# Column sums of V's weights on DMA transposes and GpSimd instead of TensorE, V of blocks 0 to 3 from raw rows, and the third block of x loaded ahead of z2's weights

## The chip, the core and the metric

The kernel runs on one core of a Trainium2 chip. The core has five engines with their own instruction queues: TensorE (PE, matmuls, with PEld as its weight loads), VectorE (DVE), ScalarE (ACT), GpSimd (POOL) and SyncE (SP, which here only issues DMAs). Each queue runs in the order in which it was written; queues are tied together by semaphores. The metric is device time in microseconds of one launch, the median of several runs.

## The reference

Two branches read the same layer-normalized input; both are added to x. S is 2048 rows, D 512, 32 heads of 16; branch A attends to 8 rows at distance 0, 2, ... 14.

```python
def _A_ref(x, wqkv, wo):
    qkv = (x @ wqkv).reshape(B, S, 3, H, Dh).transpose(2, 0, 3, 1, 4)
    q, k, v = (qkv[0], qkv[1], qkv[2])
    ...
    logits = jnp.einsum('bhsd,bhswd->bhsw', q, kg) * scale
    logits = jnp.where(mask[None, None, :, :], logits, -1000000000.0)
    attn = _softmax(logits, axis=-1)
    o = jnp.einsum('bhsw,bhswd->bhsd', attn, vg)
    return o.transpose(0, 2, 1, 3).reshape(B, S, D) @ wo

def _B_ref(x, w_in, w_sp, b_sp, w_out):
    z = _gelu(jnp.einsum('bsd,df->bsf', x, w_in))
    z1 = z[..., :Fh].copy()
    z2 = _layernorm(z[..., Fh:], axis=-1)
    g = jnp.einsum('ts,bsf->btf', w_sp, z2) + b_sp[None, :, None]
    return jnp.einsum('bsf,fd->bsd', z1 * g, w_out)
x = A_x
xn = _layernorm(x, axis=-1)
return x + _A_ref(xn, A_wqkv, A_wo) + _B_ref(xn, B_w_in, B_w_sp, B_b_sp, B_w_out)
```

V can be had without the normalized rows: with W the V columns of wqkv, m and r the mean and the reciprocal deviation of a row, (x - m) r W = r (x W) - m r (column sums of W). The kernel uses this for the first blocks.

## The kernel before

**How it is built.** The program is a list of tasks. Each task names its engine, an estimate of its duration, a priority and what it reads and writes; dependencies follow from that (and from overlaps of memory, since buffers share places in one SBUF arena). `Plan.schedule` lays all tasks out by a model with those estimates (a matmul by columns, a DMA by bytes, landing times of the first loads from a table `land`), always picking the task that can start first, and by priority among those within `tol`. The order that comes out is written to each engine's queue and is fixed: on the chip a task that is not ready holds up all behind it. `overlap` is what the model takes off every DVE operation. A hand-written chain (L1003 to L1012) fixes the order of the opening on PE, DVE and ACT.

**How it is tiled.** The 2048 rows are 16 blocks of 128 and 4 stages of 512 (index j or tc).

- x blocks are loaded (L514, L541); DVE takes each block's statistics (L599, L601, L609), GpSimd the power -1/2 (`rstd`, L611), DVE normalizes (L623). The transpose of the normalized block goes through PE and an ACT copy for blocks 0 to 3 (`xTr`, L579, and `xTe`, L587), and through a DMA transpose on SP for blocks 4 to 15 (L617).
- V (`v_block`, L645): 4 matmuls of 512 columns a block (L654). Blocks 0 and 1 take x raw: transposed on PE (`xTx`, L579), copied by ACT (`xTc`, L606), multiplied, then corrected by the column sums (`fix`, DVE, L660, in place in PSUM) and scaled by r on eviction (`Ve`, ACT, L663). The column sums come from four matmuls with a matrix of ones (`colsum`, L638) and one negating eviction to all partitions (L642). V goes from a slot (`Vn`, 8 slots, block b uses slot b mod 8) to a DRAM buffer by a store on POOL's queue (`Vw`, L668), and comes back gathered at 8 distances in the attention (L930).
- z2 (`z2_block`): 8 matmuls of 448 columns a block (L766), in two halves, as the weights are loaded in two halves (L524, L530). Gelu (L774) and sum of squares (L779) on ACT. `z2_wave` normalizes four blocks at a time: small DVE operations (L785 to L792), the power -1/2 on GpSimd (L795), and DVE's scaling (L798).
- Q and K (`qk_pair`, L677, evictions L686); products of Q with shifted K and their sums on DVE (L698, L703); the reduction over heads on PE (L713) for two stages at once, softmax on DVE and ACT (L725 to L752).
- z1 (L812, gelu L818 into `z1T`), the mixing with w_sp (L907, with w_sp transposed by DMA on SP, L880), attention times V on DVE (L935 to L941), its transposes (L944), and the output (L963, L972, L978, L983).

**Order around the change.** Loads at the start: x0 and x1 on ACT's queue; on SP the V weights in two halves, x2, z2's weights in two halves, x3 to x7, Q's and K's weights, x8 to x15. PE starts with eight matmuls on constants (L560), then the hand-written order.

Of the kernel before, what the change touches and what calls it, by code (L numbers as in the profile page):

```python
# [36 lines left out]
class Plan:  # L37
# [85 lines left out]
    def schedule(self, dma_bw=300.0, xbar_bw=190.0, dma_lat=1300.0, dma_pre=400.0, issue=None, tol=40.0, land=None,  # L123
# [49 lines left out]
        while left:  # L173
# [43 lines left out]
            if t.dma is not None:  # L217
                iss = issue[e]
                t.eng_end = r + iss
                bw = xbar_bw if t.dma.get("xbar") else dma_bw  # L220
                xs = max(r + iss + dma_pre, dma_free)
                xe = xs + t.dma["nbytes"] / (bw if xs > 7000.0 else min(bw, 265.0))
                dma_free = xe
                t.end = xe + dma_lat
                if t.name in land:
                    t.end = land[t.name]
                    dma_free = land[t.name] - 500.0
            else:
                dur = t.est
                if t.tbl is not None:  # L230
                    if tbl is not None and t.tbl != tbl:
                        dur += 1300.0
                    tbl = t.tbl
                t.end = r + dur
                t.eng_end = t.end - (overlap if e == "dve" else 0.0)
# [103 lines left out]
def build_kernel(nc, A_x, A_wqkv, A_wo, B_x, B_w_in, B_w_sp, B_b_sp, B_w_out, out, report=False, emit=True):  # L339
# [12 lines left out]
    NWARM = 8  # L352
# [3 lines left out]
    vscr = nc.dram_tensor("vscr", (16 + S, 512), BF).ap()  # L356

# [4 lines left out]
    def place(size, **names):  # L362
        for k, o_ in names.items():
            off[k] = top[0] + o_
        top[0] += size
# [5 lines left out]
    place(3584, w_in1=0, tg=0, On=2048, xcT=0, ncs=1024)  # L371
# [8 lines left out]
    off["xn"] = off["attn"]  # L380
    AR = top[0]
# [4 lines left out]
    for name, n in (("prime", 4), ("mx", 128), ("Zb", 256), ("Z", 128), ("maskt", 128), ("st6", NB * 6),  # L386
                    ("mv", NB * 2), ("vpe", NB), ("rstd", NB), ("s1", NB), ("s2", NB), ("m2", NB), ("msq", NB),
                    ("vpe2", NB), ("rstd2", NB), ("mhalf", 4)):
        foff[name] = fb
        fb += n  # L390
# [5 lines left out]
    with ExitStack() as es:  # L396
# [59 lines left out]
        for s_ in range(2):  # L456
            R1(("wv", s_), "wv", 1024, 1024 * s_)
# [8 lines left out]
        for hf in range(2):  # L466
            for b in range(2):
                R1(("xcT", b, hf), "xcT", 256, 512 * b + 256 * hf)
            R(("xnT", 0, hf), "sb", [(off["xnT"] + dc * S, off["xnT"] + dc * S + 128) for dc in (2 * hf, 2 * hf + 1)])
        R1("ncs", "ncs", 1024)  # L470
# [6 lines left out]
        def c_mm(n):  # L477
            return max(26.0, n / 2.4 + 2.7)
# [12 lines left out]
        def dma(eng, fn, nbytes, chan, reads=(), writes=(), name="", xbar=False, prio=0.0, after=()):  # L491
            return T(eng, fn, reads=reads, writes=writes, name=name, prio=prio, after=after,
                     dma=dict(chan=chan, nbytes=nbytes, xbar=xbar))
# [7 lines left out]
        ncs = A("ncs", 1024).bitcast(F32)  # L501
# [15 lines left out]
        def ld_wv(hf):  # L517
            dma("sp", lambda e: e.dma_start(AC(off["wv"] + 1024 * hf, [[512, 2], [1, 512]]),  # L518
                                            A_wqkv[256 * hf:256 * hf + 256, 1024:1536].rearrange("(c p) n -> p c n",
                                                                                               p=128)),  # L520
                256 * 512 * 2, ("wv", hf), writes=[("wv", hf)], name="ldwv%d" % hf)
# [13 lines left out]
        def ld_wqk(which, eng):  # L535
# [5 lines left out]
        dma("act", lambda e: e.dma_start(A("xin", 512), x2[0:128, :]), 128 * 512 * 2, ("xin", 0),  # L541
            writes=[("xin0", 0), ("xin0", 1)], name="ldx0")
        ld_x(1, "act")
        ld_wv(0)
        ld_wv(1)
        ld_x(2, "sp")
        ld_win2a()
        ld_win2b()
        ld_x(3, "sp")
# [23 lines left out]
        def pe_tr(src, keys, name):  # L573
            bk = plan.bank(name)

            def tr(t):
                last = None
                for dc in range(4):
                    last = t.matmul(P(bk, 128, 128 * dc), src[:, 128 * dc:128 * dc + 128], ident, start=True,  # L579
                                    stop=True)  # L580
                return last
            T("pe", tr, reads=keys + ["ident"], writes=[bk], est=(430.0 if name == "xTx0" else 4 * c_mm(128)), name=name)
            return bk
# [9 lines left out]
        def ln_block(b):  # L593
# [9 lines left out]
            if b < 2:  # L603
                bc = pe_tr(xin, xk, "xTx%d" % b)
                for hf in range(2):
                    T("act", (lambda hf: lambda a: a.activation(A("xcT", 256, 512 * b + 256 * hf), P(bc, 256, 256 * hf),  # L606
                                                                ACTF.Copy))(hf),
                      reads=[bc], writes=[("xcT", b, hf)], est=c_act(256), name="xTc%d_%d" % (b, hf), prio=-1)
# [22 lines left out]

        def colsum():
            bk = plan.bank("cs")
            for hf in range(2):
                def mm(t, hf=hf):
                    last = None
                    for dc in (2 * hf, 2 * hf + 1):
                        last = t.matmul(P(bk, 512), ones[:, 0:128], A("wv", 512, 512 * dc), start=(dc == 0),  # L638
                                        stop=(dc == 3))
                    return last  # L640
                T("pe", mm, reads=[("wv", hf)], writes=[bk], est=2 * c_mm(512) * (1 if hf else 2), name="cs_%d" % hf, prio=2)
            T("act", lambda a: a.activation(ncs, P(bk, 512), ACTF.Copy, scale=-1.0), reads=[bk],  # L642
              writes=["ncs"], est=c_act(512), name="cse", prio=-0.5)

        def v_block(b):  # L645
# [4 lines left out]
            for hf in range(2):  # L650
                def mm(t, hf=hf):
                    last = None
                    for dc in (2 * hf, 2 * hf + 1):
                        last = t.matmul(P(bk, 512), A("xcT", 128, 512 * b + 128 * dc) if b < 2 else xTv(b, dc),  # L654
                                        A("wv", 512, 512 * dc), start=(dc == 0), stop=(dc == 3))
                    return last
                T("pe", mm, reads=[("xcT", b, hf) if b < 2 else ("xnT", b), ("wv", hf)], writes=[bk],
                  est=2 * c_mm(512) * (1.5 if (b, hf) == (0, 0) else 1), name="V%d_%d" % (b, hf), prio=(2 if b < 4 else 60 + b))
            if b < 2:
                T("dve", lambda v: v.scalar_tensor_tensor(P(bk, 512), ncs, Fv("mv", 1, 2 * b), P(bk, 512),  # L660
                                                          ALU.mult, ALU.add),
                  reads=["ncs", ("mv", b)], writes=[bk], est=690, name="fix%d" % b, prio=1)
            T("act", lambda a: a.activation(vn.rearrange("p (d h) -> p d h", d=16),  # L663
                                            PC(bk.col(), [[1, 16], [16, 32]]), ACTF.Copy,
                                            scale=Fv("rstd", 1, b) if b < 2 else 1.0),
              reads=[bk] + ([("rstd", b)] if b < 2 else []), writes=[("Vn", sl)], est=c_act(512), name="Ve%d" % b,
              prio=4)
# [158 lines left out]
        lnd = [ln_block(b) for b in range(2)]  # L826
        colsum()
        v_block(0)
        v_block(1)
        lnd += [ln_block(b) for b in range(2, NB)]  # L830
# [18 lines left out]
        for b in range(2, NB):  # L849
            v_block(b)  # L850
# [152 lines left out]
        for names in (["warm%d" % wi for wi in range(NWARM)] +  # L1003
                      ["xTx0", "cs_0", "V0_0", "xTx1", "cs_1", "V0_1", "xTr0", "V1_0", "xTr1", "V1_1",
                       "z2_0_0", "z2_0_0b", "z2_0_1", "xTr2", "z2_1_0", "z2_1_1", "V2_0", "V2_1", "xTr3", "z2_2_0"],
                      ("rstd4", "Vw0"),
                      ("bnst0", "bnag0", "vpe0", "bnst1", "bnag1", "vpe1", "norm0", "norm1", "bnst2", "bnag2",
                       "vpe2", "norm2", "fix0", "bnst3", "bnag3", "vpe3", "fix1", "norm3", "bnst4", "bnag4", "vpe4",
                       "bnst5"),
                      ["bnst%d" % b for b in range(5, NB)],  # L1010
                      ("xTc0_0", "xTc0_1", "xTc1_0", "xTc1_1", "xTe0_0", "xTe0_2", "cse", "xTe1_0", "xTe2_0", "z2g0",
                       "Ve0", "xTe3_0", "z2g1", "Ve1", "Ve2", "z2s0"), ("V10_1", "Q3_3")):  # L1012
            for n0, n1 in zip(names, names[1:]):
                if byname[n0] not in byname[n1].deps:
                    byname[n1].odeps.add(byname[n0])

        plan.schedule(tol=50.0, dma_bw=300.0, dma_lat=1600.0, overlap=40.0,
                      land=dict(ldx0=3580.0, ldx1=4700.0, ldwv0=4050.0, ldwv1=5300.0, ldx2=5700.0, ldwin2a=6950.0, ldwin2b=8250.0,
                                ldx3=8650.0, ldx4=9050.0, ldx5=9400.0, ldx6=9750.0, ldx7=10200.0, ldq=11700.0, ldk=13200.0))
# [50 lines left out]
```

## Time and profile before

| what | us |
|---|---|
| runs (three) | 237.56, 237.21, 237.30; median 237.3 |
| the profiled execution's span | 236.1 |
| PE busy | 231.7 (98%) |
| DVE busy | 207.4 (88%) |
| ACT busy | 96.5 (41%) |
| POOL busy | 32.7 (14%) |
| mixing matmuls, L907 | 96.6 |
| Q and K matmuls, L677 | 28.7 |
| z2 matmuls, L766 | 26.0 |
| V matmuls, L654 | 15.6 |

The profile is one execution. A timeline row gives the start, the duration, the engine and line, output and inputs with shapes, the number of merged instructions, and in brackets the idle time before and what ended it. A matmul row's duration runs from the first start to the modelled end of the last; the pace is read from the starts. The granted TensorE clock is full in all 40 slices. The column "to landing" of a DMA counts from its issue. A few matmul records are missing.

### The profile page before, as it was taken

The numbers are of one execution on the slowest core, as the hardware profiler recorded it, in microseconds if no ns is written. First come the engines' busy times: TensorE is split into PE (matmuls) and PEld (weight loads), VectorE is DVE, ScalarE is ACT, GpSimd is POOL, SyncE is SP. The second block draws the span as 40 slices with busy tenths as digits, with TensorE's granted clock in tenths as the row PEclk, the third lists the DMA queues.
The fourth block names the chain that finished last, engine by engine and source line by source line (L and its number), as shares of the span: only waits on it lengthen the run. The fifth ranks groups of instructions, "written<-read, shape, count | busy, mean of one in ns | idle before, by whom it ended". The sixth has DMA issues, their size and how long they took to land.

```text
span 236.1 us, 2974 instructions
## 1 busy us (share of the span) xinstructions
PE 231.7 (98%) x1114; PEld 109.1 (46%) x1135; DVE 207.4 (88%) x269; ACT 96.5 (41%) x145; POOL 32.7 (14%) x56
## 2 busy tenths in 40 slices
PE   8999999999999999999999999999999999999996
PEld 3455555555444444444444444444444444444443
DVE  3799899999998899999699998986989997999432
ACT  3598889888967895510120531111111111000000
POOL 2259650311733100000000000000000000000000
PEclk9999999999999999999999999999999999999999
DMA  7998969991048325430999999998995959936432
GB/s 211 352 283 163 243 146 217 195 202 44 22 165 260 92 85 69 104 118 0 226 347 252 225 266 180 200 304 187 346 258 175 261 161 303 193 95 181 135 96 69
DMA packets 82013, 43.86 MB, mean 186 GB/s; under 512 B 54336, under 2 KB 81360, under 8 KB 82000
## 3 DMA queue, kind: packets, MB, share of 16 engines
q1 hardware_dynamic: 80768, 41.27, 71.5%
q0 software_dynamic: 800, 2.11, 2.8%
q10 hardware_dynamic: 432, 0.30, 0.6%
q8 instruction: 9, 0.15, 0.3%
q14 instruction: 4, 0.03, 0.1%
HBM read 26.35 MB, written 4.21 MB: 129 GB/s over the span
## 4 chain that ended last, share of the span: by engine, by line
PE 94%; DMA 3%; SPq 1%; ACT 1%; issue 1%; DVE 0%
PE ps L907 41%; PE ps L677 12%; PE ps L972 10%; PE ps L812 10%; PE ps L766 9%; PE ps L963 6%; PE ps L654 5%; DMA arena<-in_B_w_in_dram 3%; PE ps L713 1%; ACT arena L774 0%; SPq L518 0%; ACT arena L587 0%; PE ps L579 0%; SPq L514 0%; SPq L524 0%
## 5 line engine op out<-in xcount | busy, mean ns | idle before, releaser
L907 PE MATMUL ps<-arena 128*128 128x512 bf16 x439 | 96.6, 379 | 0.5
L907 PEld LDWEIGHTS ps<-arena 128*128 128x128 bf16 x448 | 43.7, 98 | 53.1 <-issue 0.4
L915 ACT ACTIVATE arena<-ps 128x1024 bf16<-128x1024 f32 (+1 forms) x16 | 14.7, 917 | 78.0 <-PE ps L907 78.0
L698 DVE TENSOR_TENSOR arena<-arena 128x4096 bf16<-128x4096 bf16 x16 | 36.5, 2282 | 0.1
L935 DVE TENSOR_TENSOR arena<-arena 128x4096 bf16<-128x4096 bf16 x16 | 36.4, 2283 | 0.0
L938 DVE TENSOR_TENSOR arena<-arena 128x2048 bf16<-128x2048 bf16 (+1 forms) x32 | 29.9, 948 | 0.0
L677 PE MATMUL ps<-arena 128*128 128x512 bf16 x126 | 28.7, 379 | 0.1
L703 DVE TENSOR_TENSOR arena<-arena 128x4096 bf16<-128x4096 bf16 x12 | 27.4, 2287 | 0.1
L972 PE MATMUL ps<-arena 128*128 128x512 bf16 (+2 forms) x117 | 26.9, 366 | 0.1
L766 PE MATMUL ps<-arena 128*128 128x448 bf16 x128 | 26.0, 352 | 0.5 <-DMA arena<-in_B_w_in_dram 0.5
L812 PE MATMUL ps<-arena 128*128 128x512 bf16 x110 | 24.4, 379 | 0.1
L978 DVE TENSOR_TENSOR arena<-ps,arena 128x512 bf16<-128x512 f32 (+2 forms) x17 | 11.2, 658 | 11.7 <-PE ps L972 11.7
L677 PEld LDWEIGHTS ps<-arena 128*128 128x128 bf16 x128 | 14.5, 113 | 13.0
L766 PEld LDWEIGHTS ps<-arena 128*128 128x128 bf16 x128 | 12.3, 98 | 12.7 <-ACT arena L642 0.7
L686 ACT ACTIVATE arena<-ps 128x1024 bf16<-128x1024 f32 x16 | 16.3, 1021 | 4.4 <-PE ps L677 4.1
L972 PEld LDWEIGHTS ps<-arena 128*128 128x128 bf16 x119 | 11.4, 98 | 12.8
L812 PEld LDWEIGHTS ps<-arena 128*128 128x128 bf16 x112 | 10.9, 98 | 13.2 <-ACT arena L818 0.3
L963 PE MATMUL ps<-arena 128*128 128x512 bf16 (+2 forms) x66 | 16.5, 366 | 0.1
L774 ACT ACTIVATE arena<-ps 128x896 bf16<-128x896 f32 x16 | 14.6, 914 | 3.2 <-PE ps L766 3.1
L818 ACT ACTIVATE arena<-ps 128x1024 bf16<-128x1024 f32 (+1 forms) x16 | 13.9, 923 | 4.9 <-PE ps L812 4.8
L654 PE MATMUL ps<-arena 128*128 128x512 bf16 x60 | 15.6, 379 | 0.2
L779 ACT ACTIVATE arena<-arena 128x896 bf16<-128x896 bf16 x16 | 15.1, 945 | 0.0
(61 smaller groups left out, 168.5 us busy)
## 6 DMA issues: line engine op xcount, KB each, us to landing
arena<-vscr SPq DMA_DIRECT2D x16, 1024.0 KB, 7.1
arena<-in_A_x_dram SPq DMA_DIRECT2D x30, 128.0 KB, 3.6
vscr<-arena POOLq DMA_DIRECT2D x16, 128.0 KB, 3.0
out_dram<-arena SPq DMA_DIRECT2D x15, 128.0 KB, 1.8
arena<-in_A_wqkv_dram SPq DMA_DIRECT2D x2, 512.0 KB, 6.9
arena<-in_B_w_in_dram SPq DMA_DIRECT2D x2, 448.0 KB, 6.1
arena<-in_B_w_in_dram SPq DMA_DIRECT2D x1, 896.0 KB, 5.9
arena<-in_B_w_out_dram SPq DMA_DIRECT2D x1, 896.0 KB, 4.9
```

The lines of the kernel that those rows point to most:

```text
L654: last = t.matmul(P(bk, 512), A("xcT", 128, 512 * b + 128 * dc) if b < 2 else xTv(b, dc), A("wv", 512, 512 * dc), start=(dc == 0), stop=(d ...
L677: last = t.matmul(P(bk, 512, 512 * which), AC(off["wqk"] + 2048 * which + 512 * dc + c, [[4, 128]]), AC(off["xnT"] + dc * S + 512 * j, [[1 ...
L686: T("act", lambda a: a.activation(AC(qo, [[ko - qo, 2], [1, 512]]), P(bk, 1024).rearrange("p (t n) -> p t n", t=2), ACTF.Copy, scale=0.5), ...
L698: T("dve", (lambda pbv, qb, kb: lambda v: v.tensor_tensor(pbv, qb, kb, ALU.mult))(pbv, qb, kb), reads=rd, writes=[("pb", s_)], est=c_tt(40 ...
L703: T("dve", (lambda av, bv: lambda v: v.tensor_tensor(av, av, bv, ALU.add))(av, bv), reads=[("pb", 1)], writes=[("pb", acc)], est=c_tt(4096 ...
L766: last = t.matmul(P(bk, 448, 512 * hf), xTv(b, dc), AC(off["w_in2"] + 896 * dc + 448 * hf, [[1, 448]]), start=(dc == 0), stop=(dc == 3))
L812: last = t.matmul(P(bk, 512, 512 * i), AC(off["w_in1"] + 896 * dc + 128 * fc, [[1, 128]]), AC(off["xnT"] + dc * S + 512 * j, [[1, 512]]), ...
L907: last = t.matmul(P(bk, 512, 512 * i), AC(off["z2"] + FH * sh + 128 * fc, [[1, 128]]), AC(off["wT%d" % r_] + sh * 512, [[1, 512]]), start= ...
L935: T("dve", lambda v: v.tensor_tensor(tv, tv, av, ALU.mult), reads=[("attn", b)], writes=[("Vs", sv)], est=c_tt(4096), name="pv%d" % b, pri ...
L938: T("dve", (lambda n: lambda v: v.tensor_tensor(A("Vs", n, 4096 * sv), A("Vs", n, 4096 * sv), A("Vs", n, 4096 * sv + n), ALU.add))(n), wri ...
L963: last = t.matmul(P(bk, cn), AC(off["OT"] + 512 * tb + 128 * cc, [[1, 128]]), AC(off["wo"] + 512 * cc + c0, [[1, cn]]), start=(cc == 0), s ...
L972: last = t.matmul(P(bk, cn), AC(off["z1T"] + fc * S + 128 * tb, [[1, 128]]), AC(off["w_out"] + 512 * fc + c0, [[1, cn]]), start=False, sto ...
```

## The change

- The column sums: after the twelve DMA transposes of normalized x, SP issues four more that transpose W. GpSimd adds halves nine times (256, 128, ... 1 for each of four groups) to 512 sums, stores them to a DRAM buffer (`csw`, POOL's queue), and SP loads them back to all partitions (`csr`). The matmuls with ones and their eviction are gone.
- V of blocks 0 to 3 (`NRAW`) is taken from raw x. Blocks 0 and 1 are evicted and scaled by DVE, 2 and 3 by ACT, to a float buffer `vraw`; one DVE operation a block (`fix`) later adds the column sums times -m r (`mr`, one small DVE operation) and writes the slot. The stores of V of these blocks come after that.
- The new buffers (`xcT`, `csb`, `vraw`, `wvT`, `cst`) lie in the place of `z1T`.
- Loads: x0 in two halves of rows on SP and ACT; W in three pieces; x3 directly behind x2, ahead of z2's weights. One warm-up matmul fewer.
- PE's hand-written order takes V of blocks 0 to 3 and the transposes of raw blocks 2 and 3 ahead of z2 of block 0; V of blocks 0 and 1 goes matmul by matmul. DVE's and ACT's orders follow.
- The planner: issue time and latency of DMA transposes, `tol` 20 instead of 50, DMA rate 330 instead of 300, `overlap` 20 instead of 40, a new table of landings.

```diff
@@ Plan.schedule
-                t.eng_end = r + iss
+                t.eng_end = r + (t.dma.get("iss") or iss)
...
-                t.end = xe + dma_lat
+                t.end = xe + (900.0 if t.dma.get("xbar") else dma_lat)
@@ build_kernel
-    NWARM = 8
+    NRAW = 4
+    NWARM = 7
...
     off["xn"] = off["attn"]
+    off["xcT"] = off["z1T"]
+    off["csb"] = off["xcT"] + 512 * NRAW
+    off["vraw"] = off["csb"] + 1024
+    off["wvT"] = off["vraw"] + 1024 * NRAW
+    off["cst"] = off["wvT"] + 2048
...
-                     dma=dict(chan=chan, nbytes=nbytes, xbar=xbar))
+                     dma=dict(chan=chan, nbytes=nbytes, xbar=xbar, iss=(1270.0 if nbytes < 400000 else 2200.0) if xbar else None))
...
-        dma("act", lambda e: e.dma_start(A("xin", 512), x2[0:128, :]), 128 * 512 * 2, ("xin", 0),
-            writes=[("xin0", 0), ("xin0", 1)], name="ldx0")
+        for h, q_ in enumerate(("sp", "act")):
+            dma(q_, (lambda h: lambda e: e.dma_start(ar[64 * h:64 * h + 64, off["xin"]:off["xin"] + 512],
+                                                     x2[64 * h:64 * h + 64, :]))(h),
+                64 * 512 * 2, ("xin0", h), writes=[("xin0", h)], name="ldx0%s" % "ab"[h])
         ld_x(1, "act")
-        ld_wv(0)
-        ld_wv(1)
+        for d0, dn in ((0, 1), (1, 1), (2, 2)):
+            ld_wv(d0, dn)
         ld_x(2, "sp")
+        ld_x(3, "sp")
         ld_win2a()
         ld_win2b()
-        ld_x(3, "sp")
@@ ln_block
-            if b < 2:
+            if b < NRAW:
                 bc = pe_tr(xin, xk, "xTx%d" % b)
@@ colsum
-            T("pe", mm, reads=[("wv", hf)], writes=[bk], est=2 * c_mm(512) * (1 if hf else 2), name="cs_%d" % hf, prio=2)
-            T("act", lambda a: a.activation(ncs, P(bk, 512), ACTF.Copy, scale=-1.0), reads=[bk],
-              writes=["ncs"], est=c_act(512), name="cse", prio=-0.5)
+            for dc in range(4):
+                dma("sp", (lambda dc: lambda e: e.dma_start_transpose(AC(off["wvT"] + 128 * dc, [[512, 4], [1, 128]]),
+                                                                      A("wv", 512, 512 * dc)))(dc),
+                    128 * 512 * 2, ("wvT", dc), reads=[("wv", dc)], writes=[("wvT", dc)], name="wvT%d" % dc, xbar=True,
+                    prio=2, after=lnd[4:])
+            n, prev = 256, "wvT"
+            while n:
+                if n == 256:
+                    a_, b_ = (AC(off["wvT"] + o_, [[512, 4], [1, n]]) for o_ in (0, n))
+                else:
+                    a_, b_ = (FT(o_, n) for o_ in (0, n))
+                T("pool", (lambda n, a_, b_: lambda g: g.tensor_tensor(FT(0, n) if n > 1 else Fv("cs", 4).rearrange(
+                    "p (c k) -> p c k", k=1), a_, b_, ALU.add))(n, a_, b_),
+                  reads=[("wvT", dc) for dc in range(4)] if n == 256 else ["cst"] if n == 1 else [],
+                  writes=["cst"] if n > 1 else ["cs"], est=200 + 4.2 * n, name="csum%d" % n, prio=1, after=lnr)
+                n //= 2
+            dma("pool", lambda e: e.dma_start(bass.AP(tensor=cscr.tensor, offset=cscr.offset, ap=[[1, 128], [128, 4]]),
+                                              Fv("cs", 4), allow_slow_non_contiguous=True),
+                2048, "cswr", reads=["cs"], writes=["cscr"], name="csw", prio=1)
+            dma("sp", lambda e: e.dma_start(csb, bass.AP(tensor=cscr.tensor, offset=cscr.offset, ap=[[0, 128], [1, 512]])),
+                128 * 2048, "csrd", reads=["cscr"], writes=["csb"], name="csr", prio=2)
@@ v_block
-            if b < 2:
-                T("dve", lambda v: v.scalar_tensor_tensor(P(bk, 512), ncs, Fv("mv", 1, 2 * b), P(bk, 512),
-                                                          ALU.mult, ALU.add),
-                  reads=["ncs", ("mv", b)], writes=[bk], est=690, name="fix%d" % b, prio=1)
+            if b < NRAW:
+                if b < 2:
+                    T("dve", lambda v: v.tensor_scalar(vraw(b), P(bk, 512), Fv("rstd", 1, b), None, ALU.mult),
+                      reads=[bk, ("rstd", b)], writes=[("vraw", b)], est=680, name="Ve%d" % b, prio=4)
+                else:
+                    T("act", lambda a: a.activation(vraw(b), P(bk, 512), ACTF.Copy, scale=Fv("rstd", 1, b)),
+                      reads=[bk, ("rstd", b)], writes=[("vraw", b)], est=c_act(512), name="Ve%d" % b, prio=4)
+                T("dve", lambda v: v.scalar_tensor_tensor(vdh, hd(csb), Fv("mr", 1, b), hd(vraw(b)), ALU.mult, ALU.add),
+                  reads=["csb", "mr", ("vraw", b)], writes=[("Vn", sl)], est=690, name="fix%d" % b, prio=6)
@@ the hand-written order
-                      ["xTx0", "cs_0", "V0_0", "xTx1", "cs_1", "V0_1", "xTr0", "V1_0", "xTr1", "V1_1",
-                       "z2_0_0", "z2_0_0b", "z2_0_1", "xTr2", "z2_1_0", "z2_1_1", "V2_0", "V2_1", "xTr3", "z2_2_0"],
-                      ("rstd4", "Vw0"),
+                      ["xTx0", "xTx1", "V0_0", "V0_1", "V1_0", "V1_1", "V0_2", "xTx2", "V0_3", "V1_2", "V1_3", "xTx3", "V2_0", "V2_2",
+                       "xTr0", "V3_0", "V3_2", "xTr1", "z2_0_0", "z2_0_0b", "z2_0_1", "xTr2", "z2_1_0", "z2_1_1", "xTr3", "z2_2_0"],
...
-        plan.schedule(tol=50.0, dma_bw=300.0, dma_lat=1600.0, overlap=40.0,
+        plan.schedule(tol=20.0, dma_bw=330.0, dma_lat=1600.0, overlap=20.0,
```

`hd(x)` is a view of 512 values with the head index innermost; `FT(o, n)` is n values at offset o of each of four groups of `cst`, in float.

## The prediction

> **What bounds the kernel now.** First the chain of waits by share, then in order of time; then the waits of TensorE (PE), and the timelines of the five queues.
>
> ```profile
> PE 94%; DMA 3%; SPq 1%; ACT 1%; issue 1%; DVE 0%
> ...
> 2.79 6.50 DMA arena<-in_B_w_in_dram
> ...
> 9.34 0.93 PE ps L766 x4
> ...
> PE ps L766 <- DMA arena<-in_B_w_in_dram: 0.5, 2, 0.3
> ```
>
> The end is set by one load (the second half of z2's weights, landing at 9.3 us) and, from 9.34 us to 234.2 us, by matmuls back to back. PE's only late waits are for that load. So time can be won only ahead of 9.34 us, by having done more by then; and lost anywhere behind it where PE's fixed order meets a task that isn't ready.
>
> ```profile
> 7.34 0.59 PE L654 MATMUL ps<-arena 128*128 128x512 bf16 x2
> 8.22 0.92 PE L766 MATMUL ps<-arena 128*128 128x448 bf16 x4 [0.28 <-DMA arena<-in_B_w_in_dram]
> 9.34 0.93 PE L766 MATMUL ps<-arena 128*128 128x448 bf16 x4 [0.21 <-DMA arena<-in_B_w_in_dram]
> ...
> 12.06 0.81 PE L654 MATMUL ps<-arena 128*128 128x512 bf16 x3
> ...
> 14.45 1.03 PE L654 MATMUL ps<-arena 128*128 128x512 bf16 x4
> ```
>
> These are the opening's PE rows: PE stands idle about 0.45 us ahead of 8.22 and 0.35 us ahead of 9.34, while V of blocks 2 and 3 (12.06 and 14.45; one record of the first is missing) still lies ahead. A 512-column matmul follows the last after 0.216 us (15.31 to 22.22 holds 32 of them), four transposes take 0.22 us (5.38 to 5.60), four z2 matmuls 0.75 us.
>
> **The opening.** Removed: four column-sum matmuls (0.86 us), their eviction on ScalarE (0.60 us, L642) and a 128-column warm-up. Added ahead of z2: raw transposes of blocks 2 and 3 (0.44 us) and their copies (2 x 0.60 us on ScalarE). Moved ahead: V2 and V3, 8 x 0.216 = 1.73 us. If T is the moment z2 of block 0 starts, with all data for the next tasks there, the work left at T is that left at 9.34 before, less 1.73, plus the first half of z2 (0.75). The gain is 9.34 + 1.73 - 0.75 - T = 10.32 - T. For T I walk the new order: x0 comes as two halves on two queues (first transpose at about 3.6, 3.73 before), x1 at 4.4; first copy done 0.65 + 0.3 us behind the transpose's start, as at 3.73/4.38, so V0 at 4.65, V1 at 5.35 once block 1 is copied; V0 and V1 fill the wait for x2 and x3 (to about 6.9); copies of blocks 2 and 3 end near 7.1 and 7.9, so V2 at 7.15 and V3 at 8.2; second normalized transpose to 9.3. Sum of work 1.3 + 3.46 = 4.8 us from 3.6, and 0.9 us of waits: T = 9.3. z2's weights have x3 ahead of them now, 128 KB at the 350 GB/s of those microseconds = 0.37 us: 8.5 and 9.7 us. The second half is needed at 10.06, so they no longer decide. SP issues two more descriptors there (0.46 us each), in front of loads that queue for bandwidth anyway; if landing followed issue, the halves would come at 9.4 and 10.6 and cost 0.5 us. Gain **1.0 us**, bounds 0.4 and 1.3.
>
> **Costed at nothing.** The finer V groups add no matmuls. The V0/V1 evictions on VectorE (DVE; 0.7 us each) stand where two fixes of 0.75 us stood. The four late fixes (4 x 0.75, L660's row) and a 0.16 us product add 3.2 us to DVE around 50 to 62 us; PE's order is made knowing them, and z1's matmuls (23 us of them from 73 us) fill PE meanwhile; at the far end DVE is done 9 us before it must be:
>
> ```profile
> 219.06 0.42 DVE L941 TENSOR_TENSOR arena<-arena 128x512 bf16<-128x512 bf16 x1
> ...
> 231.62 0.81 PE L963 MATMUL ps<-arena 128*128 128x384 bf16 x4
> ```
>
> Without that cover they would cost 3.2 us. The four weight transposes wait behind the twelve of normalized x on SP and push w_sp's transposes back by 4 x 1.3 us, the csr load by 0.5 us more; w_sp's eight end at 50.9 and are read from 98.2 on.
>
> **Where the column sums go.** SP issues the last x transpose at 30 us, then four at 1.3 us: until 36.5, landed about 39.5 (4.3 us from issue, the median of L617). Then nine dependent additions on GpSimd, then a store to DRAM and a broadcast load back. The adds' own time is not in the trace. They have 1024, 512, ... 4 elements per partition, 2044 in all. Low bound: DVE's 128x1024 float row, 1.22 us, so 1.1 ns an element and 0.1 us an instruction: 3.1 us. High: GpSimd's 128x128 select, 0.29 us, of which 0.10 a minimal memset's: 1.5 ns, and 0.3 us an instruction: 5.8 us. I take 4.5 (1.5, 0.9, 0.55, 0.4, and five of 0.25), midway as neither row is an add on GpSimd. The Trainium skill ("GPSIMD Engine Reference", Elementwise — side-by-side cycle accounting) gives 4497 ns for an add of 2048 float elements; by that the nine would take, by my estimate, some 6 us.
>
> But they do not run alone:
>
> ```profile
> 45.34 3.05 POOL L795 TENSOR_TENSOR fpool<-fpool 128x4 f32<-128x4 f32 x1 [10.09 <-DVE fpool L792]
> ...
> 76.62 1.04 POOL L795 TENSOR_TENSOR fpool<-fpool 128x4 f32<-128x4 f32 x1
> ...
> 45.23 2.29 DVE L703 TENSOR_TENSOR arena<-arena 128x4096 bf16<-128x4096 bf16 x1
> ...
> 76.28 1.23 DVE L730 TENSOR_TENSOR arena<-ps,fpool 128x1024 bf16<-128x1024 f32 x1
> ```
>
> The same four-element GpSimd instruction takes 1.04 us beside a DVE operation that reads PSUM, and 3.05 us beside one that reads two tensors of SBUF: 45.34 + 3.05 = 48.39 is 0.87 us behind that DVE operation's end at 47.52. It happens at 32.20 and 61.02 too, and the single rstd at 26.73 (2.53 us instead of 0.55) made DVE wait 0.52 us. From 38 to 63 us DVE does almost nothing but such 2.29 us operations. So each add waits for a boundary between two of them: nine take about 20 us instead of 4.5. The reverse, DVE waiting while GpSimd reads, four elements are too few to show: from nothing (DVE went on at once at 47.55) to all 4.5 us. As one kept the other out of reading, I take it as mutual; four adds fall there before DVE stops for another reason: 1.5 + 0.9 + 0.55 + 0.4 = 3.3 us. The Trainium skill ("SBUF — State Buffer", Who interferes with whom) says so: a DVE instruction with two SBUF inputs and a GpSimd instruction that reads SBUF lock each other out for the whole instruction; the trace agrees for GpSimd's waits, and by the rule the DVE would lose up to 6 us here, by no hold at all 3.3 us less than I sum.
>
> That other reason: L795 of wave 1 stands behind the adds on GpSimd's queue (its inputs came at 45.3, the adds' at 39.5), and DVE's L798 for blocks 4 to 7 waits for it, with the whole chain of products (L698, L703) queued behind. DVE gets there near 49.8 + 3.3 = 53 us; then GpSimd is free of it and finishes five adds (1.25), the store's issue (0.6, a V store's row) and L795 (1.04): **2.9 us** of DVE standing. Bounds: 1.6 if all adds are through, 4.5 if the store's 512 pieces cost four times 128 rows. DVE is then 6.2 us late against the plan.
>
> What is late next is the head reduction, which PE takes the moment it is planned ready:
>
> ```profile
> 60.90 2.29 DVE L703 TENSOR_TENSOR arena<-arena 128x4096 bf16<-128x4096 bf16 x1
> ...
> 64.64 1.05 PE L713 MATMUL ps<-arena 128*32 128x512 bf16 x16
> ```
>
> The last sum ends at 63.19, PE comes at 64.64: 1.45 us of slack; the planner's overlap of 20 instead of 40 ns makes some 40 DVE operations later in the plan, 0.8 us more. PE stands 6.2 - 2.25 = **3.9 us**, and nothing behind gives it back, since PE is full to the end.
>
> **Sum.** Against this execution's span of 236.1: -1.0 + 3.9 = 239.0. The median of the runs, 237.3, lies 1.2 us above that span, so 240.2.
>
> **Rivals.** (A) *The adds stay hidden*: DVE is not held, and loses under 2.25 us. For it: DVE's next operation began on time at 47.55 with a GpSimd instruction still running, and the adds' result isn't wanted till the fixes. Against: L798's place behind L795. Then only the opening counts: 237.3 - 1.0 = 236.3 (236.0 to 236.9). (B) *The fixes become the wait*: store and load back of the sums take 3.0 and 3.7 us (medians of L668 and L518); if the adds run their full 20 us with no stop at L798, they end at 61, the sums are back at 68, and DVE, due at a fix near 60, stands 8 us with 3.3 us lost before: 11.3 - 2.25 = 9 us of PE, 245.3. It decides from a landing later than some 62 us. For it: V8's slots wait for these stores too; against: a stop at L798 lets the adds finish by 54.5. (C) *No gain, no loss*: x3 lands behind 7.2, so V3 and z2 slip by 1 us and the opening's order gives nothing, or PE's stand is just 1 us: 237.3.
>
> **Chances.** Forecast 0.50 (its own range 238.2 to 243.5: lateness of 4 to 8.5 us), A 0.34, B 0.08, C 0.08. A measurement of this kernel can tell 0.2% (0.5 us) from no change: faster 0.34 (A), same 0.08 (C), slower 0.58 (forecast and B). The range 236.0 to 244.5 holds A, C and the forecast, and leaves out B and the tails.
>
> **What would show it.** Opening: V3 ahead of the first L766, which starts near 9.3 with no DMA wait at the second half. Adds: nine GpSimd instructions from 39.5 on, most about 2.3 us apart; DVE operations of 2.3 us stretched or late at the first four. Then DVE idle ahead of L798 of wave 1, released by GpSimd, and a PE gap ahead of L713. If PE has no gap behind 10 us, the forecast is wrong and A holds; if DVE's longest wait is at a fix for the sums' load, B.

## The result, and the profile after

The changed kernel takes 250.13 us (median of four runs, 249.88 to 250.20) against 237.25 us (four runs, 237.06 to 237.56): ratio 1.0538 [1.0525, 1.0552], slower. Its profiled execution has a span of 249.0 us, 12.9 us above that of before (236.1).

The chain of waits of the changed kernel by share, then TensorE's waits (us in total, times, longest):

```profile
PE 72%; DMA 9%; POOL 6%; DVE 6%; SPq 3%; issue 2%; ACT 1%; DVEq 0%; POOLq 0%
```
```profile
PE ps L814 <- ACT arena L714: 7.2, 1, 7.2
PE ps L698 <- ACT arena L714: 2.0, 1, 2.0
PE ps L761 <- DVE arena L751: 1.4, 1, 1.4
```

Before, PE was 94% of the chain and had no late wait. Now it stands three times between 62 and 84 us. L714 is ScalarE's eviction of V (L663 before), L761 the head reduction (L713 before), L751 a head sum (L703 before).

The chain of the changed kernel in order of time (start, length, what):

```profile
37.38 2.54 DMA arena<-arena
...
40.04 3.65 POOL arena L665
...
55.62 0.21 POOL fpool L665
...
56.12 10.10 DMA cscr<-fpool
...
66.24 4.37 DMA arena<-cscr
...
81.07 2.21 DVE arena L751
```

This is the path of the column sums. The last weight transpose lands at 39.92; nine adds, five of 3.65 down to 2.26 us and four of 0.21 to 0.27, end at 55.83; the store of 2 KB to DRAM takes 10.10 us from issue to landing, the load back 4.37; then come the four fixes, what DVE has queued behind them, and the head reduction.

DVE in the timeline of the changed kernel:

```profile
39.42 2.28 DVE L746 TENSOR_TENSOR arena<-arena 128x4096 bf16<-128x4096 bf16 x1
41.74 4.09 DVE L751 TENSOR_TENSOR arena<-arena 128x4096 bf16<-128x4096 bf16 x1
45.76 1.23 DVE L837 TENSOR_SCALAR fpool<-fpool 128x4 f32<-128x4 f32 x1
...
49.10 0.68 DVE L840 TENSOR_TENSOR fpool<-fpool 128x4 f32<-128x4 f32 x1
...
58.16 0.51 DVE L846 TENSOR_SCALAR arena<-arena,fpool 128x896 bf16<-128x896 bf16 x1 [3.72 <-POOL fpool L843]
...
70.63 1.13 DVE L711 SCALAR_TENSOR_TENSOR arena<-arena,fpool 128x512 bf16<-128x512 f32 x1 [6.01 <-DMA arena<-cscr]
```

Three losses of DVE are to be seen. While the adds run, its operations stretch: 4.09 us instead of 2.28, 1.23 instead of 0.17, 0.68 instead of 0.15, and one of 2.43 at 52.02 instead of 2.28: 3.55 us in all. Then it waits 3.72 us for the small power of wave 1 (L843), which stands behind the adds and the store on GpSimd's queue. Then 6.01 us at the first fix, for the sums.

TensorE in the timeline, two of its rows before the change, and the windows around its stands (busy time of PE, PEld, DVE, ACT, POOL, then granted clock, DMA share, GB/s):

```profile
10.29 0.92 PE L814 MATMUL ps<-arena 128*128 128x448 bf16 x4
11.39 0.93 PE L814 MATMUL ps<-arena 128*128 128x448 bf16 x4 [0.19 <-DMA arena<-in_B_w_in_dram]
...
62.52 1.68 PE L814 MATMUL ps<-arena 128*128 128x448 bf16 x8
66.22 1.90 PE L698 MATMUL ps<-arena 128*128 128x512 bf16 x8 [2.02 <-ACT arena L714]
...
78.79 3.17 PE L814 MATMUL ps<-arena 128*128 128x448 bf16 x8 [7.22 <-ACT arena L714]
83.33 1.05 PE L761 MATMUL ps<-arena 128*32 128x512 bf16 x16 [1.37 <-DVE arena L751]
...
87.77 23.47 PE L860 MATMUL ps<-arena 128*128 128x512 bf16 x106
```
```profile
62.17 1.68 PE L766 MATMUL ps<-arena 128*128 128x448 bf16 x8
...
74.92 23.47 PE L812 MATMUL ps<-arena 128*128 128x512 bf16 x106
```
```profile
62.00:66.00 4.00, 2.14 (x11) 0.88 (x9) 2.58 (x2) 1.35 (x2) 0.00 (x0) 1.00 0.00 0
...
74.00:78.00 4.00, 0.00 (x0) 0.00 (x0) 3.97 (x3) 0.60 (x1) 3.44 (x6) 0.65 1.20 306
78.00:82.00 4.00, 3.17 (x8) 1.01 (x8) 4.00 (x6) 3.10 (x6) 1.35 (x3) 0.50 0.67 245
```

The z2 matmuls at 62.52 stood at 62.17 before: all that happens in the first 62 us costs PE 0.35 us. The long run of z1 matmuls, at 74.92 before, starts at 87.77: 12.85 us later, which is the whole of the lost time. So it is lost between 62 and 88 us. The two waits for L714 are ways by which DVE's lateness reaches PE: at 64.65 ScalarE has waited 3.75 us for DVE (L746), with the V eviction queued behind; at 75.78 it has waited 6.72 us for the store of a block that the late fix had to write first, since V's slot is used again:

```profile
75.78 0.60 ACT L714 ACTIVATE arena<-ps 128x512 bf16<-128x512 f32 x1 [6.72 <-DMA vscr<-arena]
```

In the window from 62 to 66 the DMA engines carry nothing, though the store is in flight. After the long stand the granted clock is 0.50, and eight matmuls take 3.17 us instead of 1.68.

DVE's losses add up to this without those waits: 3.55 + 3.72 + 6.01, and the four fixes at 1.07 us where the plan had 0.69 (1.5 in all), are 14.8 us; less the 2.25 us of slack that the prediction worked out 12.5, with the opening's 0.35 some 12.9. No run measures the slack by itself; it is borne out only by the sum.

### The profile page after: what moved, and what is told of

The parts are those of the page before. It is cut to its first block, busy times and chain, and to the rows that moved or that the text cites. A ratio compares the mean times of both kernels' runs of the same rounds, so it can differ in the third digit from the quotient of the medians.

```text
span 249.0 us, 3004 instructions
## 1 busy us (share of the span) xinstructions
PE 233.0 (94%) x1117; PEld 109.1 (44%) x1138; DVE 213.7 (86%) x274; ACT 95.7 (38%) x144; POOL 45.7 (18%) x66
## 4 chain that ended last, share of the span: by engine, by line
PE 72%; DMA 9%; POOL 6%; DVE 6%; SPq 3%; issue 2%; ACT 1%; DVEq 0%; POOLq 0%
PE ps L956 39%; PE ps L860 10%; PE ps L1021 10%; POOL arena L665 6%; PE ps L1012 5%; DMA cscr<-fpool 4%; PE ps L725 3%; PE ps L814 3%; DMA arena<-in_B_w_in_dram 3%; DVE arena L751 2%; DMA arena<-cscr 2%; DVE arena L711 2%; SPq L655 2%; DMA arena<-arena 1%; PE ps L698 1%
## 5 line engine op out<-in xcount | busy, mean ns | idle before, releaser
L746 DVE TENSOR_TENSOR arena<-arena 128x4096 bf16<-128x4096 bf16 x16 | 36.7, 2292 | 0.2
L984 DVE TENSOR_TENSOR arena<-arena 128x4096 bf16<-128x4096 bf16 x16 | 36.3, 2282 | 0.0
L814 PE MATMUL ps<-arena 128*128 128x448 bf16 x128 | 27.5, 366 | 7.5 <-ACT arena L714 7.2
L751 DVE TENSOR_TENSOR arena<-arena 128x4096 bf16<-128x4096 bf16 x12 | 29.1, 2428 | 0.1
L814 PEld LDWEIGHTS ps<-arena 128*128 128x128 bf16 x128 | 12.5, 100 | 20.4 <-ACT arena L714 7.7
L665 POOL TENSOR_TENSOR arena<-arena 128x1024 f32<-128x1024 bf16 (+7 forms) x8 | 15.0, 1869 | 3.0 <-DMA arena<-arena 2.5
```

What stands on the lines that cost most here:

```text
L665: T("pool", (lambda n, a_, b_: lambda g: g.tensor_tensor(FT(0, n) if n > 1 else Fv("cs", 4).rearrange("p (c k) -> p c k", k=1), a_, b_, AL ...
L746: T("dve", (lambda pbv, qb, kb: lambda v: v.tensor_tensor(pbv, qb, kb, ALU.mult))(pbv, qb, kb), reads=rd, writes=[("pb", s_)], est=c_tt(40 ...
L751: T("dve", (lambda av, bv: lambda v: v.tensor_tensor(av, av, bv, ALU.add))(av, bv), reads=[("pb", 1)], writes=[("pb", acc)], est=c_tt(4096 ...
L814: last = t.matmul(P(bk, 448, 512 * hf), xTv(b, dc), AC(off["w_in2"] + 896 * dc + 448 * hf, [[1, 448]]), start=(dc == 0), stop=(dc == 3))
L984: T("dve", lambda v: v.tensor_tensor(tv, tv, av, ALU.mult), reads=[("attn", b)], writes=[("Vs", sv)], est=c_tt(4096), name="pv%d" % b, pri ...
```

## The experiments

All were run beside the kernel before on the same chip. The operations keep their names; line numbers move with the edits. The ratio is worked out over all runs, with a 95% interval; it need not be the quotient of the two medians.

**Column sums by matmul again, all else as changed.** This tells the sums' path from the rest of the change.

```diff
-            for dc in range(4):
-                dma("sp", (lambda dc: lambda e: e.dma_start_transpose(AC(off["wvT"] + 128 * dc, [[512, 4], [1, 128]]),
-                                                                      A("wv", 512, 512 * dc)))(dc),
...
-            n, prev = 256, "wvT"
-            while n:
...
+            bk = plan.bank("cs")
+            for hf in range(2):
+                def mm(t, hf=hf):
+                    last = None
+                    for dc in (2 * hf, 2 * hf + 1):
+                        last = t.matmul(P(bk, 512), ones[:, 0:128], A("wv", 512, 512 * dc), start=(dc == 0),
+                                        stop=(dc == 3))
+                    return last
...
+            T("act", lambda a: a.activation(csb, P(bk, 512), ACTF.Copy), reads=[bk],
+              writes=["csb"], est=c_act(512), name="cse", prio=-0.5)
```

> The changed kernel with its column sums alone undone: four matmuls with ones and one ScalarE copy give them to all partitions; the opening, the raw blocks 0 to 3 and the late fix stay. Theory (the 12.9 us come from the chain weight transposes, GpSimd additions, store, load back): the chain is gone, left are the opening's 0.35 us (matmuls from 62 us on start that much later than before) and up to 0.86 us of matmuls, so 237.5 to 238.5, no PE wait over 1 us behind 12 us. Rival (the late fixes, the shared V slots or the raw blocks themselves cost it): 245 or more.

Measured: 237.82 us against 237.05, ratio 1.0031 [1.0018, 1.0044], span 236.4. TensorE's waits have no row behind the opening. So all but 0.8 of the 12.9 us belong to the new path of the sums. Raw V for four blocks, the late fixes, the new loads, the planner's constants and the four matmuls with ones that are back cost that together, gains and losses set off.

**One DVE reduction for the nine adds.** Takes GpSimd out, keeps the store.

```diff
-            n, prev = 256, "wvT"
-            while n:
...
-                n //= 2
+            T("dve", lambda v: v.tensor_reduce(Fv("cs", 4), A("wvT", 2048).rearrange("p (c n) -> p c n", c=4), AX.X, ALU.add),
+              reads=[("wvT", dc) for dc in range(4)], writes=["cs"], est=2200, name="csum", prio=1)
```

> The nine GpSimd additions are one VectorE reduction of 2048 elements a partition (some 2.2 us); weight transposes, store, load back and late fixes stay. Theory (the additions, kept out of SBUF reads by VectorE's two-input operations, are the first 15.6 us of a chain that is wanted 13 to 14 us earlier): the sums are ready near 42 instead of 55.8, store and load end near 57, where the plan wants them; 237.7 to 239.5, and L843 of wave 1 takes 3.05 us with no wait of VectorE for it over 0.5 us. Rival (store and load set it, whatever comes before): the wait at the first fix stays 5 us or more and the time above 245.

Measured: 244.13 us, 1.0331 [1.0312, 1.0350], span 241.4. DVE's timeline, and the store in the table of DMAs (KB each, us to landing):

```profile
41.05 2.27 DVE L659 TENSOR_REDUCE fpool<-arena 128x4 f32<-128x2048 bf16 x1
...
61.13 1.12 DVE L702 SCALAR_TENSOR_TENSOR arena<-arena,fpool 128x512 bf16<-128x512 f32 x1 [4.52 <-DMA arena<-cscr]
```
```profile
cscr<-fpool POOLq DMA_DIRECT2D x1, 2.0 KB, 12.0
```

The sums are ready at 43.3, 12.5 us earlier, and no operation of DVE is stretched. Still it waits 4.52 us at the fix: the store, issued at 43.6, lands after 12.0 us, and the load comes behind a w_sp transpose on SP's queue at 56.8. So the adds are not all; the store, with a head start of 12 us, still decides. The time lies between what was expected (237.7 to 239.5) and its rival (above 245): the stop for the small power of wave 1 is gone, as expected, and most of the wait at the fix has stayed, as the rival had it.

**The same 2 KB in another layout.** The four sums of a partition go out as one piece of 16 bytes, 128 pieces instead of 512 of 4 bytes; the fix reads them back in that order. The adds stay.

```diff
-            dma("pool", lambda e: e.dma_start(bass.AP(tensor=cscr.tensor, offset=cscr.offset, ap=[[1, 128], [128, 4]]),
-                                              Fv("cs", 4), allow_slow_non_contiguous=True),
+            dma("pool", lambda e: e.dma_start(bass.AP(tensor=cscr.tensor, offset=cscr.offset, ap=[[4, 128], [1, 4]]),
+                                              Fv("cs", 4)),
...
-                T("dve", lambda v: v.scalar_tensor_tensor(vdh, hd(csb), Fv("mr", 1, b), hd(vraw(b)), ALU.mult, ALU.add),
+                T("dve", lambda v: v.scalar_tensor_tensor(
+                    vn.rearrange("p (d a e) -> p d a e", d=16, a=4), csb.rearrange("p (e d a) -> p d a e", e=8, d=16),
+                    Fv("mr", 1, b), vraw(b).rearrange("p (a e d) -> p d a e", a=4, e=8), ALU.mult, ALU.add),
```

> As the changed kernel, but the sums are stored as 128 pieces of 16 bytes instead of 512 of 4, and the fix reads them in that order. Theory (each link of the chain counts in full, as it is wanted at 57 and comes at 70.6): if the pieces are what makes the store take 10.1 us, it lands in some 3.5 us, VectorE's 6.0 us wait at the first fix goes, and the time falls by 6 to 7 us to 243 to 244.5. Rival (the store queues behind w_sp's transposes, its form is nothing): 249 to 250.5.

Measured: 245.27 us, 1.0332 [1.0305, 1.0360], span 242.7. The store's row and DVE's timeline:

```profile
cscr<-fpool POOLq DMA_DIRECT2D x1, 2.0 KB, 1.9
```
```profile
57.73 0.51 DVE L848 TENSOR_SCALAR arena<-arena,fpool 128x896 bf16<-128x896 bf16 x1 [3.51 <-POOL fpool L845]
...
64.10 1.08 DVE L711 SCALAR_TENSOR_TENSOR arena<-arena,fpool 128x512 bf16<-128x512 f32 x1
```

1.9 us instead of 10.1, and the fix waits for nothing. What is left are the forecast's own steps: DVE held 3.55 us, 3.51 us at L848 (L798 of before), PE 3.65 us at the head reduction. So the layout of a 2 KB store is worth 6.3 us of span and 4.9 us of the median. The median lies above the 243 to 244.5 that were expected; the profiled execution took 243.91, the other three 245.19 to 245.36 at a lower mean clock (0.993 instead of 1.00).

**Slots of their own for V of blocks 0 to 3.** TensorE's longest wait is named by V's slots; is that a cause, or a way?

```diff
-            vn = A("Vn" if sl < 4 else "bbc", 512, 512 * (sl % 4))
+            vn = A("xcT", 512, 512 * b) if b < NRAW else A("Vn" if sl < 4 else "bbc", 512, 512 * (sl % 4))
...
```

> As the changed kernel, but V of blocks 0 to 3 goes to four places of its own (where raw x stood), so the slots of blocks 8 to 11 wait for nobody. Theory (VectorE's lateness sets the head reduction, so PE would only stand there instead of at V's slots): PE's 7.2 us wait at L814 moves to L761 and the time stays at 248.5 to 250.5. Rival (the slots are what costs it, VectorE has room): 240 to 244.

Measured: 253.01 us, 1.0684 [1.0650, 1.0718], span 251.6. TensorE's waits:

```profile
PE ps L762 <- DVE arena L752: 12.5, 1, 12.5
```

With the slots out of the way PE stands once, at the head reduction, for the whole lateness of DVE: the wait moves and doesn't shrink. It is 2.9 us slower still, more than the 250.5 that were allowed for: the granted clock is 0.51 from 74 to 78 us and 0.50 to 86, so that the matmuls behind the stand start at half pace, and Q and K begin 1 us later than in the changed kernel, behind a wait of 0.86 us for a block of x at 4.96 us, which nothing here ties to the slots. The slots are a way, DVE's lateness the cause.

**The DVE reduction and the packed store together**, with the edits of the two above.

> Both links mended at once: one VectorE reduction instead of the nine additions, and the store in 128 pieces of 16 bytes. Everything else is as in the changed kernel. Theory (the additions' 15.6 us and the store's 10.1 us are the whole loss but the opening's 0.35 us and the fixes' 1.1 us each where the plan has 0.69): sums at 43.3, stored by 46, back by 56, no VectorE wait at the first fix, 237.3 to 238.7. Rival (a third link, the load back of the sums behind w_sp's transposes, or the fixes, still sets it): over 240.

Measured: 237.57 us (ten runs) against 237.06, 1.0018 [1.0007, 1.0029], span 236.3. The first fix in DVE's timeline has no wait:

```profile
56.94 1.14 DVE L702 SCALAR_TENSOR_TENSOR arena<-arena,fpool 128x512 bf16<-128x512 f32 x1
```

The two edits undo 12.7 of the 12.9 us of span. With only the adds gone 5.3 were left, with only the store mended 6.6: the store's share and the adds' share. The weight transposes stay in this run, and no wait of TensorE behind the opening is over 0.2 us.

**Adds that nobody reads.** The kernel of both edits, and four GpSimd adds of the old sizes behind the power of wave 1. Nothing waits for them; the DVE plan is the same. It measures the hold alone.

```diff
+            for n in (256, 128, 64, 32):
...
+                T("pool", (lambda n, a_, b_: lambda g: g.tensor_tensor(FT(0, n), a_, b_, ALU.add))(n, a_, b_),
+                  reads=[("wvT", dc) for dc in range(4)] if n == 256 else [],
+                  writes=["cst"], est=200 + 4.2 * n, name="idle%d" % n, prio=1, after=lnr)
...
+        byname["idle256"].odeps.add(byname["zr1"])
```

> The kernel with VectorE's reduction and the packed store, and beside it the first four GpSimd additions (1024 to 128 elements a partition) whose results nobody reads, queued behind L843's power of wave 1, so that nobody waits for GpSimd: what is left is that they hold VectorE out. Theory (the hold is mutual): VectorE's two-input operations beside them are stretched by 3 to 3.6 us in sum (the first from 2.28 to about 4.1), and the time is 1 to 3.5 us over that of the kernel without them. Rival (only GpSimd waits; the stretch in the changed kernel had another cause): no operation of 2.28 us is stretched by over 0.3 us, and the times agree within 0.5 us.

Measured: 241.72 us, 1.0194 [1.0166, 1.0221], span 239.4. GpSimd's and DVE's rows in the timeline:

```profile
49.16 6.39 POOL L666 TENSOR_TENSOR arena<-arena 128x1024 f32<-128x1024 bf16 x4
```
```profile
50.52 3.69 DVE L847 TENSOR_SCALAR arena<-arena,fpool 128x896 bf16<-128x896 bf16 x2
54.13 0.69 DVE L834 TENSOR_SCALAR fpool<-fpool 128x4 f32<-128x4 f32 x1
...
55.16 0.41 DVE L836 TENSOR_TENSOR fpool<-fpool 128x4 f32<-128x4 f32 x1
```

The pair of scalings takes 0.93 us without the adds, the next two rows 0.16 and 0.15: 3.55 us of hold. TensorE stands 2.35 and 0.60 us for it, and the span is 3.1 us longer than without the adds. The median is 4.15 us longer, above the 1 to 3.5 that were expected; the profiled execution has the full clock, the other three a mean of 0.993. It is the scalings that were held here, not the operations of 2.28 us that the expectation named.

**The opening as before, with both edits; and with the sums by matmul.** x0 as a whole and x2 go to ScalarE's queue and V's weights back to two pieces, so that SP issues z2's weights at 2.32 and 2.79 us as before; the planner is given the fix at 1.08 us and landing times to match.

```diff
-        for h, q_ in enumerate(("sp", "act")):
...
+        dma("act", lambda e: e.dma_start(A("xin", 512), x2[0:128, :]), 128 * 512 * 2, ("xin", 0),
+            writes=[("xin0", 0), ("xin0", 1)], name="ldx0")
...
+        ld_x(2, "act")
-        for d0, dn in ((0, 1), (1, 1), (2, 2)):
+        for d0, dn in ((0, 2), (2, 2)):
...
-        ld_x(2, "sp")
```

> The kernel with VectorE's reduction and the packed store, with another opening: x0 whole, x1 and x2 on ScalarE's queue, the V weights in two pieces, so that z2's weights are issued on SP behind three loads (as before the change) instead of six; the fix's estimate is 1.08 us. Theory (landing follows issue there: 6.5 us from issue to landing in both kernels): the second half of z2's weights lands near 9.4 instead of 11.35, z2 of block 0 starts at 9.4 to 9.8, and the time is 235.8 to 236.8, under before. Rival (it lands by bandwidth, or ScalarE's and VectorE's work sets the start of z2 at 10.3): 237.3 to 238.5.

> As the run with the matmul column sums in the changed kernel (237.82), with the opening of the previous kernel. Theory: up to 0.86 us of matmuls, part of it in gaps of the opening; 236.3 to 237.5. Rival as there: 237.8 or more.

Measured: 236.66 us (twelve runs) against 237.06, 1.0008 [0.9984, 1.0033]; by matmul 237.77, 1.0024 [1.0008, 1.0040]. The first one's PE in the timeline:

```profile
9.64 1.68 PE L805 MATMUL ps<-arena 128*128 128x448 bf16 x8
...
14.87 2.32 PE L716 MATMUL ps<-arena 128*128 128x512 bf16 x10
```

Eight z2 matmuls in one row, no wait for their weights, and Q and K at 14.87 (15.31 before, 15.87 as changed). The span of this execution is 235.5. But three of the twelve runs took 238.5 to 238.9. They hardly move the median, but the ratio takes them in, and its interval reaches to both sides of 1, so no gain can be claimed. By matmul the time falls between the 236.3 to 237.5 expected and the rival's 237.8.

**Sums earlier, and rows kept straight.** To find that spread, the weight transposes were put behind the first four x transposes; then, too, the raw rows were written in V's order.

```diff
-                    prio=2, after=lnd[4:])
+                    prio=0, after=lnd[4:8])
...
-                    T("act", lambda a: a.activation(vraw(b), P(bk, 512), ACTF.Copy, scale=Fv("rstd", 1, b)),
+                    T("act", lambda a: a.activation(vraw(b).rearrange("p (d h) -> p d h", d=16), PC(bk.col(), [[1, 16], [16, 32]]), ACTF.Copy, scale=Fv("rstd", 1, b)),
```

> The kernel with the other opening (236.66, but three of its twelve runs near 238.7), with V's weights transposed behind the first four transposes of x instead of behind all twelve: the sums are ready near 28 instead of 42, back by some 38, and no fix is near a wait. Theory (the runs near 238.7 are executions in which the sums come back behind the first fix): all runs at 236.2 to 236.9, clear of before. Rival (the spread has another source, such as the first loads): again some runs near 238.7, or 237 and more throughout, if x's later transposes are now what PE waits for.

> As the run with early sums, with the raw V kept in the order in which the fix reads it, so that of the fix's two inputs only the sums are read with a stride. Theory (the fix takes 1.08 to 1.12 us where the plan had 0.69, because its inputs are read 64 bytes apart): 0.75 to 0.95 us each; the time does not move by more than 0.3 us, as PE has slack there. Rival (the order is nothing, two float inputs of SBUF cost that): 1.08 us again.

Measured: 236.85 us, 1.0000 [0.9982, 1.0018], and 237.08 us, 0.9998 [0.9980, 1.0015], with one run of 239.0 and one of 238.3 among twelve each. The spread stays, so lateness of the sums isn't its cause, as had been supposed; what is stays open, since no profile here is of one of the long runs. The fix takes 1.106 us with straight rows and 1.120 without: the strided read of the raw rows isn't why it costs more than its 0.75. The sums are still read with a stride there, so that, and two float inputs from SBUF, remain as causes. No version beats the kernel before by more than the measurement can tell.

## Why the prediction was wrong, step by step

It forecast slower and put 240.2 us, with a range of 236.0 to 244.5; 250.13 lies outside. Every part of its mechanism was found (the hold, the stop at L798, PE's stand at the head reduction), but the largest part of the loss was not among them. By its own sign, DVE's longest wait at a fix for the sums' load, rival B holds; but B has no stop at L798.

- **The step that failed: "store and load back of the sums take 3.0 and 3.7 us (medians of L668 and L518)".** The load took 4.4, the store 10.1. The row it was priced by moves 128 pieces of 1 KB; this one moves 512 of 4 bytes. The prediction saw the 512 pieces, but charged them to the issue only ("if the store's 512 pieces cost four times 128 rows"), which took 0.94 us. With 3.0 and 3.7 the sums would have been back at 62.8, ahead of DVE's arrival at the fix at 64.6; with 10.1 and 4.4 they come at 70.6. So the wait of 6.0 us at the fix, which stood in rival B alone, came on top of the forecast's steps. Of the 9.9 us between 240.2 and 250.13 it makes 6.0; the opening makes 1.35, hold and stop 1.1, and the fixes 1.5.
- **Rival B was set against the forecast, and both happened.** "A stop at L798 lets the adds finish by 54.5" was right (55.8) and held to speak against B. B's own condition, a landing later than some 62 us, does not depend on that stop if the store is slow. Its 245.3 lacks the stop, the forecast's 240.2 the landing.
- **The adds.** Landing of the transposes 39.5, measured 39.9. Own time 4.5: from each add's end and the DVE boundary ahead of it the parts are 1.99, 1.14, 0.59, 0.32, 0.19 and then 0.27, 0.23, 0.21, 0.21 us, 5.2 in all. The rest of the 15.8 us is waiting for DVE, as forecast (20 us, had they all been caught; the last four ran while DVE stood).
- **The mutual hold, taken at 3.3 us between bounds of nothing and 4.5: 3.55.** That the size is so near is partly luck: the first four adds took 4.0 us of their own and not 3.35, and DVE lost less than all of it. The unread adds show the hold without any dependency. The Trainium skill ("SBUF — State Buffer", Who interferes with whom) says that a DVE instruction with two SBUF inputs, or one in a fast two-port mode, and a GpSimd instruction that reads SBUF exclude each other for the whole instruction. The trace agrees with the lock in both: the two-input sum at 4.09 us instead of 2.28, the scalings, of one tensor input, at 3.69 instead of 0.93; that an operation of this kind can run in such a mode is the page's word, no row shows it.
- **The stop at L798, 2.9 us (bounds 1.6 and 4.5): 3.72** (3.51 with the packed store).
- **Slack of 2.25 us, PE 3.9 us at the head reduction.** With the store packed, PE stands 3.65 us there, but that it is so near is chance: 1.81 and 0.50 us of the lateness reach it earlier, by way of V's eviction. In all the z1 run starts at 81.41, 6.5 us late; DVE's 3.55 + 3.51 + 1.5 less 2.25 gives 6.3. By this sum the slack held; the forecast lacked 0.9 us of hold and stop here (1.1 with the slow store), and the 1.5 us by which four fixes of 1.07 us exceed the plan's 0.69.
- **The opening, gain 1.0 us: a loss of 0.35.** T, the start of z2, was put at 9.3 and is 10.29; by the prediction's own formula, 10.32 - T, that leaves nothing, and the second half of z2 starts at 11.39, 0.35 us behind the end of the first (10.29 and 0.75 for its four matmuls). The stretch from 3.46 to 7.00 us has 1.7 us of work (twelve transposes, five V matmuls) and took 3.5; 0.45 and 0.57 of that are waits for V's weights. The walk allowed 0.9. And z2's second half landed at 11.35: it was issued at 4.70 instead of 2.79 and took 6.65 us (6.50 before). The landing followed the issue, the case priced at 0.5. The walk counted two more descriptors on SP ahead of these weights; there are three, and three more DMAs cost 1.9 us of issue. The run with the old order of loads shows the other side: z2 at 9.64 and Q and K 0.44 us ahead of before.
- **Costed at nothing, rightly:** the finer V groups, the DVE evictions and the stores: with the sums by matmul there is no PE wait behind the opening. The shift of w_sp was not the few us that were counted: SP stood 15.4 us for the store of the sums ahead of their load, with three of w_sp's transposes queued behind. Nothing waited for them, so it cost nothing all the same.

## What to carry to other kernels

Price a small DMA by a row with the same size of pieces, and if there is none, let its landing go into the range and ask what becomes due in that time; a layout that gives each partition one contiguous piece cost nothing here and took 8 us off the store (6 amid other DMAs). When work goes to an idle engine, count what that engine shares with the busy one and what stands behind the work on its queue: the work matters even if nobody reads its result. And two ways of being late are rivals only if one shuts out the other; where both can happen in a row, the range has to hold their sum.

## What the runs showed of the hardware

- A store of 2 KB from 128 partitions to DRAM took 10.1 us as 512 pieces of 4 bytes and 1.9 us as 128 pieces of 16 bytes in a stretch with few other transfers, 12.0 and 5.8 us amid w_sp's transposes. The number of the pieces, their size and their distance in DRAM change together; no run tells them apart. The DMA engines were recorded idle from 62 to 66 us while it was in flight, so it isn't bandwidth; what it waits for, no row shows. Two V stores issued behind it on the same queue took 9.4 us instead of the usual 3.8.
- After a stand of PE of 7.2 us the granted clock was 0.50 from 78 to 82 us, after 12.5 us it stayed so until 86 us. With the DVE reduction a stand of 3.37 us was followed by a mean of 0.57 from 68 to 72 us, where eight matmuls took 3.51 us instead of 1.89. With the packed store and a stand of 3.65 us the profiled execution kept a mean of 1.00 and took 243.91 us; the other three runs, whose stands no trace shows, had 0.993 and took 245.2 to 245.4. The Trainium skill ("TensorE: Matmul & The Clock Gate", What's actually happening) puts the clock at half after an idle window of some 3.4 us that runs freely; that a stand of 3.37 us was caught and one of 3.65 us was not agrees with it.
